# Seven half-width products for layer 1's fifth product, a third shared PSUM bank, and a new order of work

## The chip, the core and the metric

The kernel runs on one core of one Trainium2 chip. The metric is device microseconds of one execution, from the program's start to its end. The kernel before took 669.68 us as the median of three runs (668.62 to 669.77).

## What is computed

The reference runs a sparse attention over 4 batches, 8 heads, 768 positions and 64 channels. It then feeds the result, as 3072 tokens of 512 channels, to a mixture of 8 experts in which every token goes through every expert. The second half is what the change touches:

```python
out = np.zeros((N, D), dtype=np.float32)
for e in range(E):
    h = np.maximum(x @ w1[e], 0.0)     # 3072x512 by 512x1024
    ye = h @ w2[e]                     # 3072x1024 by 1024x512
    out += P[:, e:e + 1] * ye          # P: 3072x8, 8 rounds of row and column scaling
```

## The kernel before

**Two stages.** The first stage is attention, the gate and the whole of expert 0, with plain products. It lasts to about 165 us. The second is experts 1 to 7, and the change is in it alone.

**Winograd's form of Strassen.** In the second stage a product of two matrices, each cut into 2x2 blocks, is made from seven block products in place of eight. The price is sums of blocks. For the first factor the names are A11, A12, A21, A22 and the sums S1 to S4; for the second factor B11 to B22 and T1 to T4. The seven products are A11·B11, A12·B21, S4·B22, A22·T4, S1·T1, S2·T2 and S3·T3; the code numbers them 1 to 7 in this order, so that product 5 is S1·T1.

**Layer 1.** The weights of one expert are the first factor. Its hidden columns are cut into four slices i of 2x128 columns, one of each half, and its 512 channels into two halves. The tokens are cut into two halves of 1536, and each half into three blocks j of 512. Two slices (2u and 2u+1) at one j make a *duo*, so an expert has six duos (`duo`, L1032), and seven experts have 42. In a duo each of the seven products is made for both slices (k = 0 and 1), as two matmuls of 512 columns each (`product1`, L988).

**Layer 2.** The 1024 rows of four 128-token tiles at one j make four *pairs* c (`pair`, L1154). A pair is again seven products, each of four matmuls of 256 columns (`product2`, L994). On average two pairs go with one duo.

**PSUM.** Eight banks of 512 columns hold the products: two named `ab` for products 1, 2, 5 and 3, two named `g` for 6, 7 and 4 of layer 1, two `x` and two `y` for layer 2. A bank's sum goes on to its next user by ScalarE copies (`seed`, `c5`, `c2`, `c1`, `v6`) and VectorE additions (`c12`, `c22`, `v5`). ScalarE also makes the ReLUs `r11` and `r21` and the scaled parts of the output (`part`, L1249).

**A second level.** From expert 1, j = 2 on, 38 duos make product 1 for both slices in another way. The two slices, the two 128-channel chunks of the half, and two halves of the 512 tokens form a 2x2x2 block product once more, and it takes seven matmuls of 256 columns (`piece`, L1040) where the plain form takes four of 512. The steps m1, m5, m2, m6, m3, m7, m4 are those matmuls. `sd` and `c5s` are two ScalarE copies of half a bank, and `j1` and `j2` two VectorE *joins* that add half a bank to the copy. The sums that this needs are made by `wa_sum` (weights, per expert and u) and `xa_sum` (tokens, once per j).

**Weights and results.** GpSimd's queue, POOL, issues the loads of the next expert's weights (`load_w1` L198, 128 KB per transfer and two per slice; `load_w2` L211, 1 MB). It also issues the accumulating stores of the results (`da` L1270, `db` L1273) and, for expert 6, the sums in memory (`dc`, L1276). Expert 1 is different: it adds into the tile `out_acc` and stores it whole. The later experts use only rows 0 to 3 and 12 to 15 of `out_acc`, and the last block of expert 7 fetches rows 8 to 11 and 20 to 23 back. VectorE makes the Strassen sums of each weight (`w1_sum`, `w2_sum`, `wa_sum`) once it has landed. Each engine works through its queue in order, so a sum that waits for a load holds up everything behind it.

**What sets the order.** The order of every engine is fixed when the program is built. `Plan` (L30) lays out all steps by its own table of costs (`us`), by the time that it assumes a load to need (`weights`: 2.5 us; `w2`: 8.0 us), and by a table of priorities, `PR` (L1452). The order that it finds is written into the queues, and on the chip the queues run by semaphores alone.

Of the kernel before, what the change touches and what calls it, by code (L numbers as in the profile page):

```python
# [140 lines left out]
def kernel(  # L141
# [778 lines left out]
    if True:  # L920
# [79 lines left out]
        def psum(tag):  # L1000
            return fps.tile([128, 512], FP32, tag=f"{tag}{plan.now.pop(0)}", name=f"p{tag}", bufs=1)
# [5 lines left out]
        def moving1a(what, j):  # L1007
            t = slice(256 * j, 256 * (j + 1))
            if what in ("T1", "T2", "T4"):
                return xa["T1 T2 T4".split().index(what)][:, t]  # L1010
            o = 512 * j + (256 if what in ("B12", "T3", "B22") else 0)
            return xT[:, int(what in ("B21", "B22")), o:o + 256]

        def xa_sum(j, n):
            m = {w: moving1a(w, j) for w in "B11 B12 B21 B22 T1 T2 T3 T4".split()}
# [16 lines left out]
        def duo(e, j, u):  # L1032
# [7 lines left out]
            def piece(bank, lo, a, b, start=False):  # L1040
                nc.tensor.matmul(B[bank][:, lo:lo + 256], lhsT=weight1a(a, e, u), rhs=moving1a(b, j),  # L1041
                                 start=start, stop=True, skip_group_check=True)

            def m1():
                B["a0"] = psum("ab")
                piece("a0", 0, "A11", "B11", True)

            def sd():
                B["a1"] = psum("ab")
                nc.scalar.copy(out=B["a1"][:, 0:256], in_=B["a0"][:, 0:256])  # L1050

            def m5():
                piece("a0", 256, "S1", "T1")

            def c5s():
                B["m5"] = single("m5", (128, 256), late)
                nc.scalar.copy(out=B["m5"][:], in_=B["a0"][:, 256:512])

            def m2():
                piece("a0", 0, "A12", "B21")  # L1060

            def m6():
                piece("a1", 0, "S2", "T2")

            def j1():
                plus(B["a0"][:, 256:512], B["a1"][:, 0:256], B["m5"][:])

            def m3():
                piece("a0", 256, "S4", "B22")

            def m7():
                piece("a1", 0, "S3", "T3")

            def j2():
                plus(B["a1"][:, 256:512], B["a1"][:, 0:256], B["m5"][:])

            def m4():
                piece("a1", 0, "A22", "T4")

            for f in (m1, sd, m5, c5s, m2, m6, j1, m3, m7, j2, m4):  # L1080
                out[f.__name__] = f
# [72 lines left out]
        def pair(e, j, c, spare=False, tail=False, c1_at=None):  # L1154
# [17 lines left out]

            def q1():
                if spare:
                    B["x"] = psum("ab")
                    B["y"] = psum("g")
                else:
                    for x in "xy":
                        B[x] = xps.tile([128, 512], FP32, tag=f"{x}{plan.now.pop(0)}", name=f"p{x}", bufs=1)
                product2(e, c, at(0), h(A11), "B11", True)  # L1180
# [11 lines left out]
            def v5():  # L1192
                plus(at(2), at(1), B["c1"])
# [93 lines left out]
            def z3():  # L1287
                nc.scalar.activation(out=out_acc[:, 4 + c, 0:DH], in_=at(3), func=AF.Copy, scale=P_sb[:, ta, e:e + 1])
# [10 lines left out]
            def z4():  # L1299
                nc.gpsimd.tensor_tensor(out=out_acc[:, ta, DH:DM], in0=out_acc[:, ta, DH:DM], in1=out_acc[:, 4 + c, 0:DH], op=ALU.add)  # L1300
# [24 lines left out]
        def plan_duo(e, j, u, prio, split, begin, free, wt, x, put=put):  # L1325
# [9 lines left out]
            if split:  # L1335
                k5 = Buffer("m5")
                t = lambda n: [U["wa", e, u, n]]
                op("m1", "PE", us["m"], w[0] + begin + split, [a[0]])
                op("sd", "ACT", us["half"], ["m1"], [a[1]], [a[0]])
                op("m5", "PE", us["m"], ["m1"] + t(0), (), [a[0]])  # L1340
                op("c5s", "ACT", us["half"], ["m5"], [k5], [a[0]])
                op("m2", "PE", us["m"], ["sd"], (), [a[0]])
                op("m6", "PE", us["m"], ["sd"] + t(1), (), [a[1]])
                op("j1", "DVE", us["join"], ["m6", "c5s"], (), [*a, k5])
                op("m3", "PE", us["m"], ["j1"] + t(3), (), [a[0]])
                op("m7", "PE", us["m"], ["j1"] + t(2), (), [a[1]])
                op("j2", "DVE", us["join"], ["m7"], (), [a[1], k5])
# [327 lines left out]
```

## Time and profile before

| what | value |
|---|---|
| median of three runs | 669.68 us |
| the profiled execution's own time | 672.02 us |
| its span, first to last instruction | 668.8 us |
| TensorE busy | 656.2 us (98%) |
| ScalarE busy | 515.6 us (77%) |
| VectorE busy | 472.9 us (71%) |
| GpSimd busy | 261.3 us (39%) |
| mean granted TensorE clock | 0.999 |

A matmul's busy time includes its way through the array (273 ns for 256 columns, 379 ns for 512), while the next one starts after 109 or 216 ns. So TensorE counts as busy even where it loses a little time between two matmuls, and the distance between starts tells more than the share. The idle time that the profile puts before an instruction is what is left after that overlap. The profiled execution was 2.34 us longer than the median of the runs without a profile. Its span leaves 3.2 us of its own time for what lies around the first and last instruction.

### The profile page before, as it was taken

How to read it: one execution, taken by the hardware profiler on the slowest of the kernel's cores; microseconds unless marked ns; L12 is line 12 of the kernel's file. 1: busy time of each engine (PE TensorE's matmuls, PEld its weight loads, DVE VectorE, ACT ScalarE, POOL GpSimd, SP SyncE). 2: the span in 40 equal slices, each digit the busy share in tenths (PEclk: the TensorE clock that was granted, in tenths of full speed). 3: DMA queues.
4: the chain of work that ended last, by engine and by line, in shares of the span. 5: the costliest groups of instructions: out<-in, count | busy, mean ns of one | idle time of the engine just before them, and what ended most of it. 6: DMA issues, size and time to landing. Idle time of an engine off the chain costs nothing.

```text
span 668.8 us, 13968 instructions
## 1 busy us (share of the span) xinstructions
PE 656.2 (98%) x5191; PEld 446.8 (67%) x5191; DVE 472.9 (71%) x1176; ACT 515.6 (77%) x1121; POOL 261.3 (39%) x322
## 2 busy tenths in 40 slices
PE   8999999999999999999999999999999999999996
PEld 4666655555676776776767767677677676676775
DVE  7889998578899876764847576656675585664664
ACT  6776766556996678888887888888888878788771
POOL 8699504224010023434263343524343437424232
PEclk9999999999999999999999999999999999999999
DMA  9999949500735277956998497968895699978656
GB/s 162 184 151 147 141 79 88 78 2 4 139 80 130 90 141 99 138 74 98 163 120 117 68 173 109 115 107 107 134 139 74 102 169 126 155 136 152 102 81 172
DMA packets 147075, 77.67 MB, mean 116 GB/s; under 512 B 112704, under 2 KB 124736, under 8 KB 147008
## 3 DMA queue, kind: packets, MB, share of 16 engines
q0 software_dynamic: 124864, 62.64, 78.0%
q1 hardware_dynamic: 21184, 13.42, 7.9%
q8 instruction: 40, 0.66, 0.4%
q10 hardware_dynamic: 960, 0.74, 0.3%
q14 instruction: 27, 0.22, 0.1%
HBM read 55.59 MB, written 45.09 MB: 151 GB/s over the span
## 4 chain that ended last, share of the span: by engine, by line
PE 74%; issue 10%; DVE 7%; POOL 4%; DMA 3%; ACT 1%; DVEq 0%; POOLq 0%; ACTq 0%
PE px L997 16%; PE pab L991 13%; PE pg L991 13%; PE py L997 12%; PE yps L236 5%; PE hps L226 5%; PE pab L1041 3%; DMA w<-in_moe_w_dram 3%; POOL out_dram L1270 2%; POOL out_dram L1273 2%; DVE xs L552 1%; PE sg L388 1%; DMA vx<-in_v_dram 1%; PE tkq L354 1%; PE ss L475 1%
## 5 line engine op out<-in xcount | busy, mean ns | idle before, releaser
L997 PEld LDWEIGHTS <-hf 128*128 128x128 f16 x2352 | 230.1, 98 | 78.1 <-issue 0.2
L1273 POOL DMA_DIRECT2D out_dram<-out_acc x68 | 62.3, 917 | 180.1 <-ACT out_acc L1249 165.9
L941 DVE CUSTOM_DVE_ANT_0 hf<-pg,c 128x512 f16<-128x512 f32 x84 | 57.5, 684 | 104.9 <-ACT c L1100 104.6
L997 PE MATMUL px<-w,hf 128*128 128x256 f16 x656 | 98.4, 273 | 0.0
L997 PE MATMUL px<-ws,hf 128*128 128x256 f16 x656 | 98.3, 273 | 0.0
L997 PE MATMUL py<-w,hf 128*128 128x256 f16 x656 | 91.2, 273 | 0.0
L1270 POOL DMA_DIRECT2D out_dram<-out_acc x68 | 79.1, 1163 | 25.2 <-ACT out_acc L1249 24.9
L935 DVE TENSOR_TENSOR hf<-hf 128x1024 f16<-128x1024 f16 x126 | 83.2, 686 | 0.3
L991 PEld LDWEIGHTS <-w 128*128 128x128 f16 x520 | 50.9, 98 | 43.9 <-issue 3.0
L941 DVE CUSTOM_DVE_ANT_0 hf<-pab,c 128x512 f16<-128x512 f32 x84 | 57.9, 690 | 27.2 <-ACT c L1107 24.1
L1100 ACT COPY c<-pab 128x512 f32<-128x512 f32 x84 | 49.3, 587 | 31.9 <-DVE hf L941 27.6
L202 POOL DMA_DIRECT2D w<-in_moe_w_dram x56 | 43.4, 811 | 65.4 <-PE pg L991 58.1
L991 PEld LDWEIGHTS <-ws 128*128 128x128 f16 x504 | 49.3, 98 | 18.2 <-issue 1.0
L1249 ACT ACTIVATE out_acc<-py,P_sb 128x256 f32<-128x256 f32 x136 | 57.8, 482 | 1.9 <-PE py L997 1.7
L1092 ACT COPY pg<-pab 128x512 f32<-128x512 f32 x84 | 48.6, 580 | 6.3 <-PE pab L1041 2.6
L217 ACT ACTIVATE hf<-pg 128x512 f16<-128x512 f32 x84 | 50.3, 599 | 3.2 <-PE pg L991 2.8
L217 ACT ACTIVATE hf<-pab 128x512 f16<-128x512 f32 x84 | 46.6, 618 | 7.0 <-PE pab L991 6.9
L991 PE MATMUL pg<-xTs,w 128*128 128x512 f16 x168 | 50.0, 379 | 1.5 <-DVE hf L941 1.5
L1107 ACT COPY c<-pg 128x512 f32<-128x512 f32 x84 | 49.2, 586 | 1.4 <-DVE wa L938 0.5
L991 PE MATMUL pab<-xT,ws 128*128 128x512 f16 x168 | 50.0, 379 | 0.0
L991 PE MATMUL pg<-xT,w 128*128 128x512 f16 x168 | 50.0, 379 | 0.0
L991 PE MATMUL pg<-xTs,ws 128*128 128x512 f16 x168 | 49.8, 379 | 0.0
(176 smaller groups left out, 1235.6 us busy)
## 6 DMA issues: line engine op xcount, KB each, us to landing
out_dram<-out_acc POOLq DMA_DIRECT2D x136, 256.0 KB, 5.8
w<-in_moe_w_dram POOLq DMA_DIRECT2D x8, 1024.0 KB, 11.3
w<-in_moe_w_dram POOLq DMA_DIRECT2D x56, 128.0 KB, 4.3
out_dram<-out_acc SPq DMA_DIRECT2D x28, 256.0 KB, 2.2
vx<-in_v_dram POOLq DMA_DIRECT2D x16, 192.0 KB, 5.9
qst<-in_q_dram POOLq DMA_DIRECT2D x31, 96.0 KB, 5.2
kst<-in_k_dram POOLq DMA_DIRECT2D x24, 96.0 KB, 5.2
out_acc<-out_dram SPq DMA_DIRECT2D x8, 256.0 KB, 4.1
```

The costliest lines, as they stand in the source:

```text
L202: nc.gpsimd.dma_start(out=t[:, :, h, :], in_=moe_w1[e].rearrange("(dk p) f -> p dk f", p=128)[:, :, f:f + 128])
L217: nc.scalar.activation(out=out, in_=in_, func=AF.Relu, bias=0.0, scale=1.0)
L935: nc.vector.tensor_tensor(out=out, in0=in0, in1=in1, op=ALU.subtract)
L941: nc.vector._custom_dve(TENSOR_ADD_SAT, out=out, in0=in0, in1=in1, s0=FLT_MAX, s1=0.0)
L991: nc.tensor.matmul(bank[:], lhsT=w[:, dk, :], rhs=x[:, dk, :], start=start and dk == 0, stop=dk == KH - 1, skip_group_check=True)
L997: nc.tensor.matmul(bank, lhsT=a(f)[:, 128 * c:128 * (c + 1)], rhs=w[:, f, :], start=start and f == 0, stop=f == FH - 1, skip_group_check=True)
L1092: nc.scalar.copy(out=B["g" + K][:], in_=B["a" + K][:])
L1100: nc.scalar.copy(out=B["c5" + K][:], in_=B["b" + K][:])
L1107: nc.scalar.copy(out=B["c2" + K][:], in_=B["g" + K][:])
L1249: nc.scalar.activation(out=out_acc[:, (c, HT + c)[t == tb], k * DH:(k + 1) * DH], in_=at(src), func=AF.Copy, scale=scale[:, t, e:e + 1])
L1270: nc.gpsimd.dma_start(out=rows(ta), in_=out_acc[:, c, :], accum_op=ALU.add)
L1273: nc.gpsimd.dma_start(out=rows(tb), in_=out_acc[:, HT + c, :], accum_op=ALU.add)
```

## The change

- Product 5 (S1·T1) of both slices is now also made by seven matmuls of 256 columns, from expert 2, j = 1 on, in 34 duos. One function, `second`, builds both splits. The steps of the old one are called m1 to m7, md, mh, j1m and j2m, and those of the new one n1 to n7, nd, nh, j1n and j2n.
- The sums for the new split lie in rows of `out_acc` that are free after expert 1: the token sums in rows 4 to 6, the weight sums in rows 16 to 18, the half-bank copy `nh` in row 7. The scratch of the tail's `z3` moves to row 19.
- PSUM: `ab` has three banks and `y` has one. `y` is opened by `v5`, where `q1` opened it with `x`.
- `c5` and `c2` of slice 1 now come after those of slice 0, and `s2` waits for `r11` as `s3` does.
- The planner assumes 3.5 us for a load of a slice (before 2.5) and 11.0 us for layer 2's weights (before 8.0).
- All priorities in `PR` are new, so the order of every engine's queue is new from expert 1, j = 1 on.

```diff
--- before
+++ after
@@ -998,33 +998,39 @@
                                  start=start and f == 0, stop=f == FH - 1, skip_group_check=True)
 
         def psum(tag):
-            return fps.tile([128, 512], FP32, tag=f"{tag}{plan.now.pop(0)}", name=f"p{tag}", bufs=1)
+            n = plan.now.pop(0)
+            return (fps if n < 2 else xps).tile([128, 512], FP32, tag=f"{tag}{n}", name=f"p{tag}", bufs=1)
...
-        def weight1a(what, e, u):
+        def weight1a(g, what, e, u):
             if what in ("S1", "S2", "S4"):
-                return wa[e, u][:, "S1 S2 S4".split().index(what), :]
-            return w1s[e, 2 * u + int(what in ("A21", "S3", "A22"))][:, int(what in ("A12", "A22")), 0, :]
-
-        def wa_sum(e, u, n):
+                return wa[g, e, u][:, "S1 S2 S4".split().index(what), :]
+            i, k = 2 * u + int(what in ("A21", "S3", "A22")), int(what in ("A12", "A22"))
+            return ws1[e, i][:, 0, k, :] if g else w1s[e, i][:, k, 0, :]
+
+        def spare16(t, n):
+            return out_acc[:, t, 0:n // 2].bitcast(FP16)
+
+        def wa_sum(g, e, u, n):
             if n == 0:
-                wa[e, u] = late.tile([128, 3, 128], FP16, tag="wa", name="wa", bufs=3)
-            m = {w: weight1a(w, e, u) for w in "A11 A12 A21 A22 S1 S2 S3 S4".split()}
+                wa[g, e, u] = (spare16(HT + 4 + (2 * e + u) % 3, 384).rearrange("p (s f) -> p s f", s=3) if g else
+                               late.tile([128, 3, 128], FP16, tag="wa", name="wa", bufs=3))
+            m = {w: weight1a(g, w, e, u) for w in "A11 A12 A21 A22 S1 S2 S3 S4".split()}
             f, o, a, b = ((plus, "S1", "A21", "A22"), (sub, "S2", "S1", "A11"), (sub, "S3", "A11", "A21"),
                           (sub, "S4", "A12", "S2"))[n]
             f(m[o], m[a], m[b])
...
+            def second(g, a, x):
+                b0, b1, held = a + "0", a + "1", x + "5c"
+
+                def piece(bank, lo, w, v, start=False):
+                    nc.tensor.matmul(B[bank][:, lo:lo + 256], lhsT=weight1a(g, w, e, u), rhs=moving1a(g, v, j),
+                                     start=start, stop=True, skip_group_check=True)
+
+                def f1():
+                    B[b0] = psum("ab")
+                    piece(b0, 0, "A11", "B11", True)
+
+                def fd():
+                    B[b1] = psum("ab")
+                    nc.scalar.copy(out=B[b1][:, 0:256], in_=B[b0][:, 0:256])
+
+                def f5():
+                    piece(b0, 256, "S1", "T1")
+
+                def fh():
+                    if g:
+                        plan.now.pop(0)
+                        B[held] = out_acc[:, 7, 0:256]
+                    else:
+                        B[held] = single("m5", (128, 256), late)[:]
+                    nc.scalar.copy(out=B[held], in_=B[b0][:, 256:512])
+
+                def f2():
+                    piece(b0, 0, "A12", "B21")
+
+                def f6():
+                    piece(b1, 0, "S2", "T2")
+
+                def j1():
+                    plus(B[b0][:, 256:512], B[b1][:, 0:256], B[held])
+
+                def f3():
+                    piece(b0, 256, "S4", "B22")
+
+                def f7():
+                    piece(b1, 0, "S3", "T3")
+
+                def j2():
+                    plus(B[b1][:, 256:512], B[b1][:, 0:256], B[held])
+
+                def f4():
+                    piece(b1, 0, "A22", "T4")
+
+                for f in (f1, fd, f5, fh, f2, f6, j1, f3, f7, j2, f4):
+                    out[x + f.__name__[-1] if f.__name__[0] == "f" else f.__name__ + x] = f
+
+            second(0, "a", "m")
+            second(1, "b", "n")
...
+            def open_bank(x, other):
+                B[x] = (psum(other) if spare else
+                        xps.tile([128, 512], FP32, tag=f"{x}{plan.now.pop(0)}", name=f"p{x}", bufs=1))
+
             def q1():
-                if spare:
-                    B["x"] = psum("ab")
...
+                open_bank("x", "ab")
                 product2(e, c, at(0), h(A11), "B11", True)
 
             def c1():
@@ -1190,6 +1205,7 @@
                 product2(e, c, at(1), h(S1), "T1", False)
 
             def v5():
+                open_bank("y", "g")
                 plus(at(2), at(1), B["c1"])
 
...
+            def second(h, c, first, last):
+                kh = Buffer(h + "5")
+                t = lambda n: [split[h][n]]
+                op(h + "1", "PE", us["m"], first + split[h], [c[0]])
+                op(h + "d", "ACT", us["half"], [h + "1"], [c[1]], [c[0]])
+                op(h + "5", "PE", us["m"], [h + "1"] + t(0), (), [c[0]])
+                op(h + "h", "ACT", us["half"], [h + "5"], [kh], [c[0]])
+                op(h + "2", "PE", us["m"], [h + "d"], (), [c[0]])
+                op(h + "6", "PE", us["m"], [h + "d"] + t(1), (), [c[1]])
+                op("j1" + h, "DVE", us["join"], [h + "6", h + "h"], (), [*c, kh])
+                op(h + "3", "PE", us["m"], ["j1" + h] + t(3), (), [c[0]])
+                op(h + "7", "PE", us["m"], ["j1" + h] + t(2), (), [c[1]])
+                op("j2" + h, "DVE", us["join"], [h + "7"], (), [c[1], kh])
+                op(h + "4", "PE", us["m"], ["j2" + h] + last, (), [c[1]])
+                return ([h + "2", h + "3"], [h + "4"])
+
+            if "m" in split:
+                made_a = second("m", a, w[0] + begin, w[1])
             else:
...
+                if "n" not in split:
+                    op("p5" + K, "PE", us["p"], made_a[1] + t(0) + [x[0]], [b[k]])
+                    made_b = ["p5" + K]
+                else:
+                    if k == 0:
+                        both = second("n", b, made_a[1] + t(0) + [x[0]], [wt[i0 + 1, 0]])
+                        d["p51"] = d["n4"]
+                    made_b = both[k]
+                op("c5" + K, "ACT", us["c5"], made_b + (["c50"] if k else []), [k5], [b[k]])
                 op("p6" + K, "PE", us["p"], ["seed" + K] + t(1) + [x[1]], (), [g[k]])
-                op("c2" + K, "ACT", us["c2"], ["p6" + K], [k2], [g[k]])
+                op("c2" + K, "ACT", us["c2"], ["p6" + K] + (["c20"] if k else []), [k2], [g[k]])
...
-        xa = [late.tile([128, NH // 2], FP16, name=f"xa{n}") for n in range(3)]
-        plan.more({"x": 2, "y": 2, "c1": 1, "m5": 1})
+        xa = [[late.tile([128, NH // 2], FP16, name=f"xa{n}") for n in range(3)],
+              [spare16(4 + n, 1024) for n in range(3)]]
+        plan.more({"x": 2, "y": 1, "c1": 1, "m5": 1, "n5": 1})
+        plan.ring["ab"].append(None)
...
+            "m1": 4854.5, "m5": 3714.1, "m2": 2962.3, "m6": 2288.5, "m3": 2736.4, "m7": 4133.9,
+            "m4": 3754.0, "seed0": 3414.9, "seed1": 4905.3, "p20": 2462.8, "r110": 3485.5, "p21": 4796.1,
...
-            load(("w1", e, i), lambda: load_w1(e, i), 0.85, 2.5, deps)
+            load(("w1", e, i), lambda: load_w1(e, i), 0.85, 3.5, deps)
...
-               [bx, by])
+               [bx])
             op("c1", "ACT", us["c1"], ["q1"] + ([src[1]["c121"], src[1]["c221"]] if spare else []), c1s, [bx])
             op("q5", "PE", m, ["q1", W2[e, 0]] + of("s1"), (), [bx])
-            op("v5", "DVE", us["v5"], ["q5", "c1"], (), [bx, by] + c1s)
+            op("v5", "DVE", us["v5"], ["q5", "c1"], [by], [bx] + c1s)
...
-                split = None
-                if (e, j) >= (1, 2):
-                    split = [U["wa", e, u, m] for m in range(4)] + [XA[j, m] for m in range(4)]
+                    xa_sums(0, 2, base + 100)
+                split = {}
+                for g, h, since in ((0, "m", (1, 2)), (1, "n", (2, 1))):
+                    if (e, j) >= since:
+                        split[h] = [U["wa", g, e, u, m] for m in range(4)] + [XA[g, j, m] for m in range(4)]
...
+                if n == 7:
+                    p5s = ("p50", "p51")
+                    held = [pairs[1, 1, c]["landed"] for c in range(4)]
+                    for v in range(2):
+                        wa_sums(1, 2, v, base + 30 + 10 * v, held + users(2, 0, v, p5s))
+                    for m, i in enumerate((1, 2, 0)):
+                        xa_sums(1, i, base + 50 + 70 * m, held + users(*((2, 0) if i == 0 else (1, i)), 0, p5s)
+                                + users(*((2, 0) if i == 0 else (1, i)), 1, p5s))
                 if e + 1 < E:
                     w = base + PR["w"]
                     if k == 2:
-                        load(("w2", e + 1), lambda: load_w2(e + 1), 0.9, 8.0, pair_users(e - 1, 2))
+                        load(("w2", e + 1), lambda: load_w2(e + 1), 0.9, 11.0, pair_users(e - 1, 2))
...
-                        wa_sums(e + 1, 0, w - 90, users(e - 1, 2, 1))
+                        for g in (0, 1) if e > 1 else (0,):
+                            wa_sums(g, e + 1, 0, w - 90, users(e - 1, 2, 1))
...
```

More of the change, by code (lines that the diff above doesn't have):

```diff
@@ L1038, in h @@
                 return B["h"][:, q, :, :] if k is None else B["h"][:, q, k, :]
[L1040 to L1069, printed above, removed]
@@ L1287, in z3 @@
             def z3():
-                nc.scalar.activation(out=out_acc[:, 4 + c, 0:DH], in_=at(3), func=AF.Copy, scale=P_sb[:, ta, e:e + 1])
+                nc.scalar.activation(out=out_acc[:, HT + 7, c // 2 * DH:(c // 2 + 1) * DH], in_=at(3), func=AF.Copy, scale=P_sb[:, ta, e:e + 1])
             def z2():
@@ L1299, in z4 @@
             def z4():
-                nc.gpsimd.tensor_tensor(out=out_acc[:, ta, DH:DM], in0=out_acc[:, ta, DH:DM], in1=out_acc[:, 4 + c, 0:DH], op=ALU.add)
+                nc.gpsimd.tensor_tensor(out=out_acc[:, ta, DH:DM], in0=out_acc[:, ta, DH:DM], in1=out_acc[:, HT + 7, c // 2 * DH:(c // 2 + 1) * DH], op=ALU.add)
             def x0():
@@ L1334, in plan_duo @@
             w = [[U["w1", e, i0 + k]] for k in range(2)]
[L1335 to L1347, printed above, removed]
-                op("m4", "PE", us["m"], ["j2"] + w[1], (), [a[1]])
-                made_a, begun = (["m2", "m3"], ["m4"]), ["m4"]
+            def second(h, c, first, last):
[15 more added lines that the diff above has]
+                made_a = second("m", a, w[0] + begin, w[1])
             else:
@@ L1472, in w_sums, with wa_sums @@
                                   [WT.get((e, i, n - 1)), U["w1", e, i], *old], prio + 0.01 * n)
[L1474 removed]
+        def wa_sums(g, e, u, prio, old=()):
             for n in range(4):
[L1476 to L1478 removed]
+                U["wa", g, e, u, n] = put("DVE", us["wa"], lambda n=n: wa_sum(g, e, u, n),
+                                          [U.get(("wa", g, e, u, n - 1)), *old]
+                                          + [WT[e, 2 * u + k, 2] for k in range(2)], prio + 0.01 * n)
         def w2_sums(e, ns, prio, old=()):
```

52 lines of the change are left out of this document (17 added, 35 removed), and 16 rows, old and new, of the table PR.

## The prediction

> **What bounds the kernel now.** I read the busy table first, then windows of 50 us, then the chain that ended last in one duo, then TensorE's waits, and last the two engines that feed it.
>
> ```profile
> PE 656.2 (98%) x5191; PEld 446.8 (67%) x5191; DVE 472.9 (71%) x1176; ACT 515.6 (77%) x1121; POOL 261.3 (39%) x322
> ```
>
> TensorE is at 98%. The windows (columns: window, length, then busy us and count of each engine, granted clock, DMA share, GB/s) show where the others have room:
>
> ```profile
> 206.00:218.00 12.00, 12.00 (x89) 8.44 (x87) 11.93 (x36) 7.43 (x17) 1.49 (x2) 1.00 0.52 129
> ...
> 300.00:350.00 50.00, 50.00 (x360) 35.07 (x359) 30.94 (x64) 42.67 (x101) 20.56 (x26) 1.00 0.88 125
> ...
> 550.00:600.00 50.00, 49.01 (x355) 34.60 (x354) 30.55 (x71) 41.54 (x98) 24.37 (x29) 1.00 0.90 131
> ```
>
> From 300 to 350 us, ScalarE is busy 85% and VectorE 62%. In one early stretch, VectorE is busy 99%, and TensorE still has no gap. The chain that ended last consists of TensorE alone here (start, length, what):
>
> ```profile
> 399.18 0.87 PE px L997 x8
> 400.05 0.43 PE pab L991 x2
> ...
> 401.78 0.22 PE pab L1041 x2
> 402.00 0.44 PE px L997 x4
> ...
> 411.23 0.87 PE px L997 x8
> ```
>
> The same step comes back after 12.05 us, one duo. Two matmuls of 512 columns take 0.432, four of 256 take 0.437, a half-width piece 0.109. A duo's 24, 56 and 7 of them sum to 12x0.432 + 14x0.437 + 7x0.109 = 12.06. So there is no lost time in a steady duo: TensorE's own work is the bound. It does lose time in three places:
>
> ```profile
> 173.48 0.69 DVE L935 TENSOR_TENSOR ws<-w 128x1024 f16<-128x1024 f16 x1 [0.99 <-DMA w<-in_moe_w_dram]
> ...
> 174.83 0.59 PE L991 MATMUL pab<-xT,w 128*128 128x512 f16 x2 [0.77 <-DVE hf L941]
> ```
> ```profile
> 541.43 0.69 DVE L935 TENSOR_TENSOR ws<-w 128x1024 f16<-128x1024 f16 x1 [1.93 <-DMA w<-in_moe_w_dram]
> ...
> 545.64 0.59 PE L991 MATMUL pg<-xTs,w 128*128 128x512 f16 x2 [0.47 <-DVE hf L941]
> ```
> ```profile
> 580.62 0.29 DVE L938 TENSOR_TENSOR ws<-w 128x256 f16<-128x256 f16 x1 [4.32 <-DMA w<-in_moe_w_dram]
> ...
> 582.96 0.59 PE L991 MATMUL pg<-xTs,w 128*128 128x512 f16 x2 [0.99 <-DVE hf L941]
> ```
>
> Each time a weight sum stands in VectorE's queue before its load has landed, and a ReLU addition behind it is late for TensorE. A 512-column matmul is shown as 0.163 us longer than the distance to the next (0.379 against 0.216), so the losses are 0.93, 0.63 and 1.15 us, together 2.7.
>
> **The change, part by part.**
>
> *The fifth product.* Per duo four matmuls of 512 columns (0.863) go and seven of 256 (0.764) come: -0.099 us. 34 duos: **-3.4 us**, all on the path, as steady TensorE has no gap.
>
> *Its helpers on ScalarE.* Two half-bank copies per duo, shown as 0.36 and 0.39 us long. Followed by another instruction, a copy of this size holds ScalarE for about 0.29. That is 0.58 on top of the 10.2 us that 85% of 12.06 makes: 10.8 of 11.96, 90%. It has room.
>
> *Its helpers on VectorE.* Two joins per duo at 0.43 us, 0.33 when followed by another, are +0.67; 48 weight sums at 0.14 and 12 token sums at 0.2 us are 9 us, or 0.3 per duo. 7.5 us per duo become 8.4, 70%. It has room in a steady duo.
>
> *The hand-overs.* Here a wait is added, so I laid the new order of a steady duo beside TensorE's distances. From the end of n6 to n3 TensorE has a pair of 512s and four 256s, 0.87 us. The join between needs 0.163 for the array, 0.04 to start (a copy starts 0.04 after the last matmul's shown end), 0.43 for itself and 0.06 to release TensorE: 0.69. That leaves 0.19. From n7 to n4: 0.86 against 0.69, 0.18. VectorE is idle before both joins. For `mh` the cover from m5 to m2 is 0.98. `md` and `mh` run behind each other and need 0.163 + 0.04 + 0.29 + 0.39 + 0.06 = 0.94, so 0.04 is left, the least of all. `c2` before product 7 has 0.07 and 0.10. The same reckoning gives 0.14 as the least of a steady duo before. All are above nothing, so I take **0**. If what I laid out is 0.1 us off, four hand-overs miss by 0 to 0.06, up to 0.1 per duo (3.4 us).
>
> *The first duos.* VectorE was busy 99% there. In the new order expert 2's weight sums stand in one unbroken row with ReLU additions and expert 1's output additions. From the output addition that a pair's last product releases to the `v5` that TensorE wants, there are seven additions into `out_acc` (0.39 apart when in a row), ten weight sums (1.8), four ReLU additions (0.61), two Strassen sums (0.6), one `v5` and one join (0.33 each), then this `v5` itself (0.43) and its release: 9.4 us. TensorE has 8.7 us of work in that time, so it waits about 0.7. An earlier VectorE row at expert 1, j = 1 is late by 0.3. Before, four small waits of 0.14 to 0.18 (one is the join that ended at 222.92, for a matmul that could have started at 222.87) came to 0.6 in this stretch. The first sums in the spare rows wait for expert 1's stores of those rows, with ReLU additions queued behind them; these stores stand 14 us of work ahead and land in 2.2 us (median), so that wait costs 0. Net **+0.7**, at least 0 (new waits no longer than the old), at most 2 (both rows late by twice as much).
>
> *The later sums.* In the new order VectorE comes to expert 2's `w2` sum some 5 us later than before, and for the later experts 13.5 us of work lie between the issue of a `w2` load and its sum. The median landing is 11.3 us, the longest 11.8; before, VectorE stood waiting from 8.1 us (first place) and 9.9 us (second) after the issue on. Between a slice's second transfer and its sum lie at least 5.7 us after the first expert; at the third place it took 5.4. `dc` no longer stands between `da` and the loads waiting for an earlier store, so the last loads are issued earlier too. I take all three waits as gone: **-2.7 us**, bounds 0 and -2.7.
>
> One rule speaks against this. Where VectorE was busiest (206 to 218 us, 99%), the two loads of a slice took 0.75 us each to issue, the shortest of all, and landed after 3.2 to 3.6 us (median of all: 4.3); the longest, 6.1, came at 563 us, among stores. The Trainium skill, "SBUF — State Buffer", section "Who interferes with whom", says that a VectorE instruction with two SBUF inputs contends with a GpSimd instruction that reads SBUF, and its summary that descriptor generation starves while VectorE is in its fast modes. By that rule the 60 added sums would hold up GpSimd's issues and make loads later; the trace does not bear it out for sums of this kind.
>
> *The rest.* The third `ab` bank and the single `y` bank add no instruction; what they cost is in the waits above. In the tail, TensorE's last eight matmuls, then `z3`, `z4`, `z2`, `z0`, `x0`, `x1` and the store keep their order (TensorE ended at 662.5 of 668.8 us), so the last 6.3 us stay. The two ordering waits on slice 1 and on `s2` hold steps that came later anyway. These cost 0.
>
> Sum: 668.8 - 3.4 - 2.7 + 0.7 = 663.4 us of span, 666.6 us as the profiled execution's own time (672.02 - 5.4). The median of the runs shown is 2.34 us below that execution. Part of that difference may be late loads that only a profiled run has, so of the 2.7 I count 2.3 on the median's scale: 669.7 - 3.4 - 2.3 + 0.7 = **664.7 us**.
>
> **The rivals.**
>
> *The loads stay late.* Stores and loads share the DMA engines, and the new order may just move the crowd; GpSimd's issues held up by VectorE's added sums would have the same effect. For it: the slice loads of 6.1 us at 563 us; against it: the added distance, and the short issues at 206 to 218 us. 669.7 - 3.4 + 0.7 = 667.0.
>
> *Hand-overs miss, slower.* ScalarE at 90%, in a fixed order, lets `md`, `mh` and `c2` slip; TensorE waits in every one of 34 duos. It decides from (3.4 + 2.3 - 0.7)/34 = 0.15 us per duo on. At 0.3 (two joins and one copy late by 0.1 each, as that join at 222.92 was) it is 10.2 us: 664.7 + 10.2 = 674.9. At 0.1 to 0.15 it is 668.1 to 669.8, no change. For it: 0.04 of room at `mh`. Against it: before, 12.05 us per duo with ScalarE at 85%, no loss at all.
>
> *VectorE bounds more of the start.* Expert 2's new weight and token sums (8 to 19 us after that row) add to a VectorE that was 88% busy from 200 to 250 us. If that loses 3 us more: 667.7.
>
> The split may also do nothing to TensorE's sum; but the built order has 504 half-width pieces (266 before, and 34x7 = 238 more) and 888 matmuls of 512 columns (1024 before, and 34x4 = 136 less), so I give that no chance.
>
> **How the numbers follow.** 0.2% (1.3 us) is about what a measurement of this kernel can tell from no change. Forecast 0.65 (own range 663 to 666.5); late loads 0.12 (0.02 of it by VectorE's added sums); a slower start 0.07, of which 0.03 are within 0.2%; hand-overs 0.16, of which 0.05 are within 0.2% and 0.11 slower. Faster 0.65 + 0.12 + 0.04 = 0.81, same 0.08, slower 0.11. The range starts at 662.8 (669.7 - 3.4 - 2.7 with nothing lost at the start is 663.6, less 0.8 for the spread of runs, whose lowest lies 1.1 below the median). It ends at 668.8, past the late loads, the slower start and 0.1 us per duo at the hand-overs (664.7 + 3.4), and leaves out the slower cases and the extremes.
>
> **What the changed profile would show.** The same px step back after 11.95 to 12.0 us in a steady duo; seven pieces at 0.11 twice per duo; no VectorE sum that waits over 0.5 us for a load, and no TensorE wait at 541 to 583 us; one or two waits of TensorE for a `py` addition before 220 us, under 1 us each. A duo of over 12.1 us, with TensorE waiting for a half-bank copy, a join or `c2`, would make me wrong.

## The result, and the profile after

The changed kernel takes 665.25 us (median; 664.45 to 665.98) against 669.72 us for the kernel before in the same series. The ratio is 0.9935, with a 95% interval of 0.9918 to 0.9953. A second series, on the chip of the last experiment, gave 665.21 against 669.58: 0.9927, interval 0.9907 to 0.9948. The change saves about 4.4 us, 0.66%. The forecast was 664.7 us.

The profiled execution of the changed kernel took 664.45 us, with a span of 662.7 us. That span is 6.1 us shorter than the one shown of before, more than the median spans differ: these are 667.4 us (47 executions of before in the later series) and 663.5 us (the four of the changed kernel). The profiled span of before, 668.8 us, lies 1.4 us above its median, and that of the changed kernel 0.8 us below.

The busy table of the changed kernel:

```profile
PE 652.9 (99%) x5293; PEld 456.8 (69%) x5293; DVE 506.0 (76%) x1304; ACT 533.2 (80%) x1189; POOL 260.0 (39%) x322
```

TensorE has 102 more matmuls (34 x 7 - 34 x 4) and 3.3 us less busy time. VectorE has 33 us more to do and ScalarE 18 us more.

Three windows of the same trace (window, length, then busy us and count of TensorE, its weight loads, VectorE, ScalarE and GpSimd, granted clock, DMA share, GB/s):

```profile
206.00:218.00 12.00, 11.79 (x85) 8.10 (x84) 11.55 (x31) 7.35 (x16) 1.49 (x2) 1.00 0.56 138
300.00:350.00 50.00, 50.00 (x379) 36.85 (x377) 33.64 (x67) 45.26 (x110) 20.48 (x25) 1.00 0.89 122
550.00:600.00 50.00, 50.00 (x379) 36.77 (x377) 34.22 (x86) 45.50 (x110) 25.12 (x30) 1.00 0.95 139
```

ScalarE is busy 90.5% and VectorE 67% in the steady stretch, and TensorE has no gap. The stretch from 550 to 600 us, where it lost 1 us before, is full as well. The first window is now the one with a gap.

The chain that ended last, over one duo (start, length, what):

```profile
405.42 0.87 PE py L997 x8
406.29 0.43 PE pab L991 x2
406.72 0.33 PE pab L1050 x3
...
408.79 0.22 PE pab L1050 x2
...
417.38 0.87 PE py L997 x8
```

TensorE alone carries it, the half-width pieces are 0.11 each, and the same step comes back after 11.96 us (12.05 before).

To see where TensorE loses time, I laid the starts of its matmuls beside the sum of their own distances (0.216 us per 512 columns, 0.109 per 256), from the first `px` on. That own sum is 493.9 us before and 490.6 after. In the profiled executions TensorE ends 3.67 us behind it before, and 1.27 us after. Before, 2.72 of the 3.67 are the three late loads (0.93, 0.63, 1.16). After, 0.98 are lost up to 213 us and 0.29 later, most of it in three places (0.07 to 0.10 each). The rest of the 6.1 us (0.3) is in the first stage.

### The profile page after: what moved, and what is told of

Same layout as the page of the kernel before. It is cut to its first block, busy times and chain, and to the rows that moved or that the text cites. A ratio compares the mean times of both kernels' runs of the same rounds, so it can differ in the third digit from the quotient of the medians.

```text
span 662.7 us, 14448 instructions
## 1 busy us (share of the span) xinstructions
PE 652.9 (99%) x5293; PEld 456.8 (69%) x5293; DVE 506.0 (76%) x1304; ACT 533.2 (80%) x1189; POOL 260.0 (39%) x322
## 4 chain that ended last, share of the span: by engine, by line
PE 89%; DVE 8%; DMA 1%; issue 0%; ACT 0%; DVEq 0%
PE px L997 21%; PE pg L991 16%; PE py L997 16%; PE pab L991 12%; PE pab L1050 8%; PE yps L236 5%; PE hps L226 5%; DVE xs L552 1%; DMA kT<-kst 1%; PE sg L388 1%; PE idle L597 1%; PE tkq L354 1%; DVE em L440 1%; DVE km L382 1%; PE pab L997 1%
## 5 line engine op out<-in xcount | busy, mean ns | idle before, releaser
L1289 POOL DMA_DIRECT2D out_dram<-out_acc x68 | 60.0, 883 | 209.3 <-ACT out_acc L1265 193.1
L1265 ACT ACTIVATE out_acc<-py,P_sb 128x256 f32<-128x256 f32 x136 | 61.2, 476 | 24.2 <-PE py L997 21.6
L941 DVE CUSTOM_DVE_ANT_0 hf<-pab,c 128x512 f16<-128x512 f32 x84 | 57.8, 689 | 25.8 <-ACT c L1123 12.4
L1286 POOL DMA_DIRECT2D out_dram<-out_acc x68 | 69.0, 1014 | 20.4 <-ACT out_acc L1265 19.4
L938 DVE TENSOR_TENSOR pab<-pab,out_acc 128x256 f32<-128x256 f32 x68 | 29.3, 431 | 43.9 <-PE pab L1050 43.9
L938 DVE TENSOR_TENSOR py<-px,c 128x256 f32<-128x256 f32 x82 | 35.0, 427 | 35.9 <-PE px L997 34.9
L991 PE MATMUL pab<-xT,w 128*128 128x512 f16 x184 | 54.6, 380 | 0.0
L1108 ACT COPY pg<-pab 128x512 f32<-128x512 f32 x84 | 50.4, 601 | 2.7 <-PE pab L1050 2.7
L217 ACT ACTIVATE hf<-pab 128x512 f16<-128x512 f32 x84 | 50.4, 601 | 2.4 <-PE pab L991 1.8
```

The source lines that it names most:

```text
L217: nc.scalar.activation(out=out, in_=in_, func=AF.Relu, bias=0.0, scale=1.0)
L938: nc.vector.tensor_tensor(out=out, in0=in0, in1=in1, op=ALU.add)
L941: nc.vector._custom_dve(TENSOR_ADD_SAT, out=out, in0=in0, in1=in1, s0=FLT_MAX, s1=0.0)
L991: nc.tensor.matmul(bank[:], lhsT=w[:, dk, :], rhs=x[:, dk, :], start=start and dk == 0, stop=dk == KH - 1, skip_group_check=True)
L1108: nc.scalar.copy(out=B["g" + K][:], in_=B["a" + K][:])
L1265: nc.scalar.activation(out=out_acc[:, (c, HT + c)[t == tb], k * DH:(k + 1) * DH], in_=at(src), func=AF.Copy, scale=scale[:, t, e:e + 1])
```

## The experiments

All times are medians; each ratio is to the kernel before on the same chip. The last two columns are from the profiled execution: TensorE's own sum from the first `px` on, and how far it ends behind it. The series were run on several chips, so the ratio compares two kernels more safely than the medians do; the medians of before were 669.20 to 669.72 us.

| kernel | us | ratio (95% interval) | own sum, us | behind, us |
|---|---|---|---|---|
| before | 669.72 | 1 | 493.9 | 3.67 |
| changed | 665.25 | 0.9935 (0.9918 to 0.9953) | 490.6 | 1.27 |
| changed, once more | 665.21 | 0.9927 (0.9907 to 0.9948) | 490.6 | 1.70 |
| fifth product not split | 677.37 | 1.0119 (1.0106 to 1.0132) | 493.9 | 10.28 |
| n1 twice | 668.92 | 0.9995 (0.9987 to 1.0004) | 494.3 | 1.32 |
| before, new load times | 667.65 | 0.9975 (0.9966 to 0.9984) | 493.9 | 0.80 |
| changed, old load times | 673.60 | 1.0067 (1.0053 to 1.0082) | 490.6 | 9.98 |
| copy ahead of `mh` | 671.58 | 1.0031 (1.0019 to 1.0043) | 490.6 | 8.11 |
| copy behind the seed | 665.08 | 0.9931 (0.9918 to 0.9943) | 490.6 | 2.83 |
| first join twice | 677.69 | 1.0126 (1.0113 to 1.0139) | 490.6 | 14.01 |
| banks as before | 710.7 | 1.0621 (1.0606 to 1.0637) | 490.6 | not comparable |
| `w2` assumed 12.5 us | 667.01 | 0.9954 (0.9938 to 0.9969) | 490.6 | 3.58 |

My theory was that TensorE's own work bounds every duo, and that the gain is fewer columns plus loads that no longer come late. The main rivals were that the gain is only one of the two, and that the added helpers bind.

### The fifth product not split

```diff
-                for g, h, since in ((0, "m", (1, 2)), (1, "n", (2, 1))):
+                for g, h, since in ((0, "m", (1, 2)), (1, "n", (E, 0))):
...
-                if n == 7:
+                if n == -1:
...
-                        for g in (0, 1) if e > 1 else (0,):
+                        for g in (0,):
```

> The changed kernel with the fifth product never split (its token and weight sums are not made either); the third bank, the new priorities and the new assumed load times stay, and the order is planned anew with them. My theory: TensorE's own sum grows by the 34 x 0.099 = 3.4 us again, the load waits stay gone, and the order laid out beside TensorE's distances is late by at most 0.9 us at a few places. So 665.3 + 3.4 = 668.7 us (667.8 to 669.6), a steady duo of 12.05 to 12.06 us, and no VectorE sum that waits over 0.5 us for a load. Rival 1, the gain is that of the order and the loads and the added helpers eat what the pieces save: 664.8 to 666. Rival 2, the pieces are the whole gain and the load waits were a matter of the profiled execution alone: 669.7, with load waits of 0.9 us and more back in the trace.

Measured: 677.37 us, 7.7 us above the highest of the expected values. TensorE's own sum did grow by 3.4 us. The other 9.0 us are new waits. The order was planned anew, for less work with priorities meant for more, which is the likely cause, though no run separates it from the rest. The same places return in each expert. One of them, in the timeline:

```profile
390.58 0.69 DVE L941 CUSTOM_DVE_ANT_0 hf<-pab,c 128x512 f16<-128x512 f32 x1 [5.18 <-ACT out_acc L1265]
391.19 0.68 DVE L941 CUSTOM_DVE_ANT_0 hf<-pg,c 128x512 f16<-128x512 f32 x1
391.31 0.58 ACT L1123 COPY c<-pg 128x512 f32<-128x512 f32 x1 [0.38 <-DVE hf L941]
391.94 0.59 PE L991 MATMUL pg<-xT,w 128*128 128x512 f16 x2 [0.41 <-ACT c L1123]
```

VectorE stands idle for 5.18 us, until a ScalarE output part has ended. Then two ReLU additions, a ScalarE copy and TensorE follow late. With the helpers gone and TensorE's work as in the kernel before, this kernel is slower than that one, so this run can't price the pieces alone. My expectation overlooked that a lateness in a periodic order is paid once per expert. The next run keeps the order.

### The first piece twice

```diff
                     piece(b0, 0, "A11", "B11", True)
+                    if g:
+                        piece(b0, 0, "A11", "B11", True)
```

> The changed kernel with the first piece of the split fifth product computed twice in each of the 34 duos (the second overwrites the first with the same numbers); order, banks, helpers and loads as they are. TensorE gets 34 x 0.109 = 3.7 us more, nearly what its fewer columns save. My theory, TensorE's own sum decides in every duo and nothing else moves: ratio to the changed kernel's 665.3 us of 669.0 (+3.7, 668.6 to 669.4), a steady duo of 12.07 us, TensorE's waits as in the changed kernel. Rival, the gain came with the order and the loads and TensorE's columns are not what counts: 665.3 to 666.

Measured: 668.92 us, 3.67 above the changed kernel, for 3.71 us of added TensorE work. (The two medians come from different series; by the ratios to before it is 0.0060 of 669.3, or 4.0 us.) In the profiles TensorE's own sum grows by 3.7 us and its lateness by 0.05. The chain shows the fourth piece where there were three, and the step returns after 12.07 us:

```profile
407.08 0.87 PE py L997 x8
408.39 0.44 PE pab L1050 x4
...
419.15 0.87 PE py L997 x8
```

Column for column, TensorE's time is the kernel's time. So the 3.4 us that the pieces save are worth 3.4 us here, and the rival that TensorE's columns don't count falls.

### The new load times alone, in the kernel before

```diff
-            load(("w1", e, i), lambda: load_w1(e, i), 0.85, 2.5, deps)
+            load(("w1", e, i), lambda: load_w1(e, i), 0.85, 3.5, deps)
...
-                        load(("w2", e + 1), lambda: load_w2(e + 1), 0.9, 8.0, pair_users(e - 1, 2))
+                        load(("w2", e + 1), lambda: load_w2(e + 1), 0.9, 11.0, pair_users(e - 1, 2))
```

> The kernel before with only the two assumed load times of the change (3.5 and 11.0 us). Its priorities then give nearly the order it had, so my theory, that the times act only together with the new priorities and the added work, expects the waits for loads to stay: 669.7 +- 0.8 us, with VectorE waits for loads of about 1 to 2.4 us. Rival, the assumed times alone mend the loads: 669.7 - 2.3 to 2.7 = 667.0 to 667.4 us, without a TensorE wait at 541 to 583 us.

Measured: 667.65 us, 1.55 us below before in the same series (by the interval of the ratio 1.1 to 2.3). My theory was wrong on the time and right on VectorE's waits. The rival was right on TensorE's waits, and the time came near its 667.0 to 667.4 us. VectorE still waits for the loads, but TensorE no longer does. The timeline of this kernel:

```profile
539.93 0.69 DVE L935 TENSOR_TENSOR ws<-w 128x1024 f16<-128x1024 f16 x1 [1.57 <-DMA w<-in_moe_w_dram]
...
542.95 0.69 DVE L941 CUSTOM_DVE_ANT_0 hf<-pg,c 128x512 f16<-128x512 f32 x1 [1.00 <-ACT c L1100]
...
578.12 0.29 DVE L938 TENSOR_TENSOR ws<-w 128x256 f16<-128x256 f16 x1 [2.96 <-DMA w<-in_moe_w_dram]
...
579.12 0.69 DVE L941 CUSTOM_DVE_ANT_0 hf<-pg,c 128x512 f16<-128x512 f32 x1
579.61 0.59 PE L991 MATMUL pab<-xT,ws 128*128 128x512 f16 x2
579.73 0.21 DVE L938 TENSOR_TENSOR wa<-w 128x128 f16<-128x128 f16 x1
```

And the third place in the kernel before, where the late sum stood at 580.62 us:

```profile
581.56 0.22 DVE L938 TENSOR_TENSOR wa<-w 128x128 f16<-128x128 f16 x1
...
582.23 0.68 DVE L941 CUSTOM_DVE_ANT_0 hf<-pg,c 128x512 f16<-128x512 f32 x1
```

Before, the four small `wa` sums stood between the late sum and the ReLU addition that TensorE wanted. Now the ReLU addition stands ahead of them. At the place near 540 us VectorE even waits 1.00 us for ScalarE before its ReLU addition. At the place near 173 us both ReLU additions now go first (172.41 and 173.17), and the sum follows at 179.41 without a wait. So what decides is not whether a sum waits for its load, but what is queued behind it.

### The old load times, in the changed kernel

```diff
-            load(("w1", e, i), lambda: load_w1(e, i), 0.85, 3.5, deps)
+            load(("w1", e, i), lambda: load_w1(e, i), 0.85, 2.5, deps)
...
-                        load(("w2", e + 1), lambda: load_w2(e + 1), 0.9, 11.0, pair_users(e - 1, 2))
+                        load(("w2", e + 1), lambda: load_w2(e + 1), 0.9, 8.0, pair_users(e - 1, 2))
```

> The changed kernel with the old assumed load times (2.5 us for a slice, 8.0 us for a w2) in the planner, all else as changed; the order is planned anew with them. My theory: the sums come before their loads again in several places, VectorE stands waiting for 0.5 to 0.7 us at about eleven of them and TensorE for a part of these, and the order of the first duos is late by up to 2.3 us: 665.3 + 2 to 3 = 667.3 to 668.3 us, a steady duo still 11.96 us. Rival, the added work between loads and sums alone moves them far enough and the assumed times do nothing: 665.3 +- 0.7.

Measured: 673.60 us, 8.3 us above the changed kernel and three times what I expected. The rival falls. About half (4.6 us) is lost up to 229 us, where the order of the first duos is worse and only one load is late (0.59 us at 173.9). Another 4.9 us are six places where a join stands behind a `w2` sum that waits for its load. The timeline at one of them:

```profile
356.00 0.29 DVE L938 TENSOR_TENSOR ws<-w 128x256 f16<-128x256 f16 x1 [2.38 <-DMA w<-in_moe_w_dram]
356.21 0.42 DVE L938 TENSOR_TENSOR pab<-pab,out_acc 128x256 f32<-128x256 f32 x1
...
356.69 0.27 PE L1050 MATMUL pab<-xTs,out_acc 128*128 128x256 f16 x1 [1.22 <-DVE pab L938]
```

### One copy more on ScalarE, in two places

Ahead of `mh`:

```diff
                         B[held] = single("m5", (128, 256), late)[:]
+                        if e >= 3:
+                            nc.scalar.copy(out=out_acc[:, HT + 7, 0:DH], in_=out_acc[:, HT + 7, DH:DM])
                     nc.scalar.copy(out=B[held], in_=B[b0][:, 256:512])
```

> The changed kernel with one copy added that computes nothing (256 columns, SBUF to SBUF, on ScalarE) in each of the 30 duos of experts 3 to 7, put ahead of mh, the copy of the held half. It occupies ScalarE for some 0.29 us. My theory, the room ahead of this copy is 0.04 us: late by 0.25 us per duo, 30 x 0.25 = 7.5, 672.8 us (671.5 to 674), and TensorE waits named after the copy mh in each of these duos. Rival, ScalarE is busy 80% and takes a copy of 0.29 us anywhere: 665.3 +- 0.7.

Behind the seed:

```diff
                     nc.scalar.copy(out=B["g" + K][:], in_=B["a" + K][:])
+                    if e >= 3 and k == 0:
+                        nc.scalar.copy(out=out_acc[:, HT + 7, 0:DH], in_=out_acc[:, HT + 7, DH:DM])
```

> The changed kernel with the same added copy, in the same 30 duos, put behind the seed of the first half instead. ScalarE's busy time grows as much as with the copy ahead of mh. My theory, the instructions behind the seed have over 0.3 us of room: 665.3 +- 0.7 us. Rival, ScalarE at 90% of a steady duo is full by its mean, and 0.29 us more makes it the bound wherever they stand: 667 to 673 us.

Measured: 671.58 us ahead of `mh`, 665.08 us behind the seed. The same copy costs 6.3 us in one place and nothing in the other. The window of the kernel with the copy behind the seed shows ScalarE at 93% and TensorE without a gap:

```profile
300.00:350.00 50.00, 50.00 (x378) 36.82 (x377) 33.62 (x67) 46.70 (x115) 20.67 (x25) 1.00 0.88 121
```

So ScalarE's share of busy time is not the bound. Its place in the order is. The hand-over in the changed kernel, in the timeline:

```profile
402.41 0.36 ACT L1059 COPY pab<-pab 128x256 f32<-128x256 f32 x1 [0.42 <-PE pab L1050]
402.68 0.38 ACT L1070 COPY m<-pab 128x256 f32<-128x256 f32 x1
...
403.07 0.27 PE L1050 MATMUL pab<-xa,wa 128*128 128x256 f16 x1
403.18 0.27 PE L1050 MATMUL pab<-xT,w 128*128 128x256 f16 x1
```

and with the copy (L1071) ahead of `mh` (L1072):

```profile
404.98 0.36 ACT L1059 COPY pab<-pab 128x256 f32<-128x256 f32 x1 [0.42 <-PE pab L1050]
405.25 0.41 ACT L1071 COPY out_acc<-out_acc 128x256 f32<-128x256 f32 x1
405.55 0.38 ACT L1072 COPY m<-pab 128x256 f32<-128x256 f32 x1
405.64 0.27 PE L1050 MATMUL pab<-xa,wa 128*128 128x256 f16 x1
...
405.98 0.27 PE L1050 MATMUL pab<-xT,w 128*128 128x256 f16 x1
```

With the copy, `mh` ends at 405.93 and m2 starts 0.05 us later, 0.23 late. In the changed kernel `mh` ends at 403.06 and m2 at its own time, 403.18: the room, by which `mh` could end later at no cost, is 0.12 - 0.05 = 0.07 us. The copy holds ScalarE for 0.30 us, and 0.30 - 0.07 is the 0.23 that is lost. All 30 duos lose 0.20 to 0.23, together 6.7 us in the trace; the medians differ by 6.3.

In the profiled execution with the copy behind the seed, one `w2` load was late as well:

```profile
567.18 0.29 DVE L938 TENSOR_TENSOR ws<-w 128x256 f16<-128x256 f16 x1 [1.96 <-DMA w<-in_moe_w_dram]
567.39 0.42 DVE L938 TENSOR_TENSOR pab<-pab,out_acc 128x256 f32<-128x256 f32 x1
...
567.87 0.27 PE L1050 MATMUL pab<-out_acc,ws 128*128 128x256 f16 x1 [1.24 <-DVE pab L938]
```

It cost 1.4 of that execution's 2.83 us. The changed kernel has the same place: there the wait was 0.57 us in one profiled execution and 1.00 in the other, at a cost of 0 and 0.4 us.

### The first join twice

```diff
                     plus(B[b0][:, 256:512], B[b1][:, 0:256], B[held])
+                    if g:
+                        plus(B[b0][:, 256:512], B[b1][:, 0:256], B[held])
```

> The changed kernel with the first join of the split fifth product done twice on VectorE in the 34 duos (same inputs, same result). It occupies VectorE for 0.33 us more. My theory, the hand-over from n6 to n3 has a room of 0.1 to 0.19 us: late by 0.14 to 0.25 us per duo, 5 to 9 us, 670 to 674 us, with TensorE waits named after the join. Rival, VectorE at 70% has room for it and the pieces of the other product cover it: 665.3 +- 0.7.

Measured: 677.69 us, 12.4 above the changed kernel, and more than expected. The trace loses 0.35 us in each duo, and 0.49 where a weight sum stands right ahead of the join. The timeline of the doubled join:

```profile
414.51 0.27 PE L1050 MATMUL pab<-out_acc 128*128 128x256 f16 x1
...
414.89 0.90 DVE L938 TENSOR_TENSOR pab<-pab,out_acc 128x256 f32<-128x256 f32 x2 [1.09 <-PE pab L1050]
415.85 0.27 PE L1050 MATMUL pab<-xTs,out_acc 128*128 128x256 f16 x1 [0.19 <-DVE pab L938]
```

and of the single one in the changed kernel:

```profile
408.74 0.27 PE L1050 MATMUL pab<-out_acc 128*128 128x256 f16 x1
...
409.12 0.43 DVE L938 TENSOR_TENSOR pab<-pab,out_acc 128x256 f32<-128x256 f32 x1 [1.09 <-PE pab L1050]
...
409.71 0.27 PE L1050 MATMUL pab<-xTs,out_acc 128*128 128x256 f16 x1
```

The single join ends at 409.55 and n3 starts at 409.71. The doubled one ends at 415.79 and n3 starts 0.06 later. So the room is 0.16 - 0.06 = 0.10 us. The second join adds 0.47 us, not the 0.33 that I took from joins in a row on different tiles, and 0.47 less 0.10 is about the loss. VectorE stands idle for 1.09 us just before this join, so its share of busy time says nothing about the hand-over either.

### The banks as before

```diff
-        plan.more({"x": 2, "y": 1, "c1": 1, "m5": 1, "n5": 1})
-        plan.ring["ab"].append(None)
+        plan.more({"x": 2, "y": 2, "c1": 1, "m5": 1, "n5": 1})
```

> The changed kernel with the banks as before: two for layer 1's products and two for the pairs' second halves, planned anew. The split fifth product then has to wait for the banks of the split first. My theory, that TensorE is the bound only as long as every hand-over is covered: in each of the 34 duos that split both, the first piece of the second split comes late by 0.5 to 2.3 us, which makes 17 to 77 us: 682 to 742 us, with TensorE waits named after copies and joins. Rival, the third bank is not needed and the gain is in the columns alone: under 668 us.

Measured: 710.1 to 711.4 us, 45.5 us above the changed kernel (by the medians), or 1.34 us for each of 34 duos, in the middle of what was expected. Its profiled execution was granted a TensorE clock of only 0.655 and took 987.5 us, so its waits can't be set beside the others in size. The largest that it names are of `pab` matmuls for half-bank copies (5.9 us in 16 waits) and for joins (2.8 us in 5), as expected. The run shows that the split, with these priorities, needs the third bank. It was planned anew like the unsplit one, so how much of the 45.5 us is the bank and how much the order stays open.

### A longer time assumed for `w2`

The late `w2` loads near 566 us suggested to plan for 12.5 us.

```diff
-                        load(("w2", e + 1), lambda: load_w2(e + 1), 0.9, 11.0, pair_users(e - 1, 2))
+                        load(("w2", e + 1), lambda: load_w2(e + 1), 0.9, 12.5, pair_users(e - 1, 2))
```

> The changed kernel once more, unaltered, on the same chip as the next one. 665.3 us (664.5 to 666); TensorE behind its own summed work by about 1.3 us, of that 0.9 before 213 us; VectorE waits of 0.4 to 2 us for the two late w2 loads near 566 and 578 us, which cost TensorE 0 to 1.4 us.

> The changed kernel with 12.5 us in place of 11.0 as the assumed time of a w2 load, planned anew; all else as changed. My theory, the w2 sums stand further behind their loads, VectorE no longer waits near 566 and 578 us, and nothing else moves, since the order laid out beside TensorE's distances is late by about as much (1.1 against 1.0 us): 664.6 to 665.3 us, 0 to 0.7 below the unaltered one. Rival, any replanning with priorities found for other assumed times makes new late hand-overs, as the old assumed times did: 667 us or more.

Measured: 665.21 us for the changed kernel and 667.01 us with 12.5. It is slower by 1.8 us, not faster. VectorE now waits 0.3 to 0.8 us for this load in four experts, and each time a join is held up. The timeline of the longest:

```profile
567.25 0.29 DVE L938 TENSOR_TENSOR ws<-w 128x256 f16<-128x256 f16 x1 [0.81 <-DMA w<-in_moe_w_dram]
...
567.99 0.42 DVE L938 TENSOR_TENSOR pab<-pab,out_acc 128x256 f32<-128x256 f32 x1
...
568.47 0.27 PE L1050 MATMUL pab<-out_acc,ws 128*128 128x256 f16 x1 [0.62 <-DVE pab L938]
```

The four places make 1.9 us. Three `w2` sums now stand ahead of the join, where it was one: the join starts 0.74 us after the first of them (567.25 to 567.99), against 0.21 in the changed kernel's order (567.18 to 567.39, above). So the planner, told that the load takes longer, put more behind the sum that waits and ahead of the join that TensorE wants. None of the variants beats the changed kernel. What TensorE still loses after 165 us is 1.3 to 1.7 us, and an order without these waits was not tried.

## Why the prediction was right, and where not

- **The fifth product, -3.4.** Right. The own sum is 3.36 us shorter (493.92 to 490.56) and the duo 11.96 us long. Adding 3.71 us back, with all else kept, costs 3.67 by the medians and 4.0 by the ratios.
- **ScalarE and VectorE have room.** Right. They are at 90.5% and 67%, and a copy more per duo behind the seed costs nothing.
- **The hand-overs, 0.** Right in the sum; two rooms were off. At `mh` 0.04 was forecast and 0.07 measured. From n6 to n3 it was 0.19 and 0.10: the join starts 0.11 us after the shown end of n6 (409.01 to 409.12), where I had taken 0.04 from a copy. The rival of missed hand-overs was close by: 0.30 us more on ScalarE at `mh`, or one more join, turns the gain into a loss (671.6 and 677.7 us).
- **The first duos, +0.7.** Too much, and by a slip: the parts that the step names, 0.7 and 0.3 less 0.6, make 0.4, and the sum carried 0.7. The parts themselves came near. Up to 255 us TensorE loses 0.99 us to small waits, against 0.63 before without the late load, so +0.36. Over the whole stage, late loads aside, I count +0.22 (1.17 - 0.95; the `w2` wait at 578 us left out). Where one wait of 0.3 and one of 0.7 were expected, there are six of 0.08 to 0.36 us: 0.32 together at 183 to 200 us, behind output and ReLU additions, and 0.65 together at 207 to 213 us, behind `py` additions and a join. The longest, in the timeline of the changed kernel, is a join that ends late, so that TensorE starts 0.36 us late; the `py` addition behind it costs another 0.11:

```profile
211.97 0.43 DVE L938 TENSOR_TENSOR pab<-pab,m 128x256 f32<-128x256 f32 x1
212.31 0.43 DVE L938 TENSOR_TENSOR py<-px,c 128x256 f32<-128x256 f32 x1
212.46 0.27 PE L1050 MATMUL pab<-xT,wa 128*128 128x256 f16 x1 [0.19 <-DVE pab L938]
...
212.79 0.60 PE L997 MATMUL py<-ws,hf 128*128 128x256 f16 x4
```

- **The later sums, -2.7, of which 2.3 on the median's scale.** The three waits are gone, but 2.3 was too much: the new load times alone gave 1.55 us, and they leave no TensorE wait for a load. The step read 2.7 off one profiled execution and took 0.4 off for the median. That execution's span is 1.4 us above the median span of before. If these 1.4 us are late loads, 1.3 of the 2.7 are left, near the 1.55; no profile of a median execution shows it. The step's reason held only in part. I had the gain come from more work between issue and sum; with the new load times in the kernel before it came from moving the wanted ReLU addition ahead of the small sums, with VectorE waiting 0.9 to 3 us all the same. And the step is not safe: two `w2` sums still wait 0.57 and 0.66 us in the profile after, and TensorE 0.10 us at 578 us, so these signs were wrong. In the second profile of the changed kernel the longest such wait is 1.00 us, and with the copy behind the seed it is 1.96.
- **The rule on SBUF contention.** "SBUF — State Buffer" of the Trainium skill, section "Who interferes with whom", has a VectorE instruction with two SBUF inputs contend with a GpSimd instruction that reads SBUF. The same section reports a probe in which `tensor_tensor`, the operation of the added sums, did not stall a DMA, and the prediction left this out. The trace agrees with the probe where VectorE is busiest: from 206 to 218 us of the changed kernel (96%) a slice's two loads are still issued in 0.74 and 0.76 us. The landings are mixed. The median of a slice went from 4.3 to 5.7 us and that of a `w2` from 11.3 to 9.5, and the DMA engines were busier (0.95 against 0.90 from 550 to 600 us). Why the slices land later stays open. The prediction also misread one number here: 6.1 us is not the longest landing of a slice before. Twelve slices issued right behind a `w2` took 8.8 to 11.6 us.

The sum with what was measured is 669.7 - 3.36 - 1.55 + 0.22 = 665.0, against 665.25. It is a rough sum: the 1.55 was measured in another order and holds some 0.15 of other small waits (0.95 against 0.80), and the late `w2` loads of the changed kernel (0.10 and 0.52 us in its two profiles) are left out. The two sizes that were off, 0.75 for the loads and 0.48 for the start, had opposite signs and cancelled in part, so that the forecast came within 0.55 us is partly luck.

## What to carry to other kernels

Where one engine has no gap, price a change by that engine's own distances, and treat the rest as hand-overs: write down the room of each in hundredths of a microsecond, because 0.3 us on an engine that is 80% busy cost nothing in one place and 6 us in another. When a wait for a load shows up, look at what is queued behind the waiting instruction before changing the load. An order written out from priorities fits only the work and the assumed times it was found for: taking the fifth product's split away again made the kernel slower than it was before.

## What the runs showed of the hardware

Two VectorE additions of 256 columns on the same tile, one after the other, take 0.89 to 0.90 us, so the second adds 0.47 us; why it is more than on different tiles no run shows. On different tiles they follow each other after 0.33 us (403.07 and 403.40 in the changed kernel, a `py` addition and the one behind it). ScalarE copies of 256 columns are shown as 0.36 to 0.41 us long and follow each other after 0.27 to 0.30. A VectorE join started 0.11 us after the shown end of the piece it waits for (409.01 to 409.12), and the next one 0.04 us after (410.09 to 410.13). I had taken one value for both.
